# Seven block products instead of eight in the last 512 tokens of a gated MLP, with paired memory units and rewritten instruction orders

## The chip, the cores and the metric

The kernel runs on one core of a Trainium2 chip. The metric is device time in microseconds for one execution. Before the change the median of three runs is 672.04 us (671.85 to 672.40).

## What is computed

Attention over 4 batches and 8 heads (576 tokens, 64 dimensions a head) is mixed with a read from a memory matrix; the result, 2304 tokens by 512, goes through a gated MLP with no nonlinearity:

```python
local = np.matmul(softmax(causal(q @ k.T / 8)), v)
q_p = phi(q)                                   # x > 0 ? x + 1 : exp(x)
mem_out = (q_p @ M_prev) / (q_p @ z_prev + 1e-6)
x = g * mem_out + (1 - g) * local              # to 2304 x 512
out = ((x @ w_a) * (x @ w_b)) @ w_out          # 512 -> 1536 -> 512
```

The weights are given in 64 bits; the kernel makes of each a high and a low part of 32 bits in the form that one matmul pass takes, and every product of the MLP is three matmuls: high by high, high by low, low by high.

## The kernel before

Engines are called PE (matmuls), DVE, ACT, POOL (GpSimd) and SP (which issues the DMAs). The first 200 us are attention. Its steps, and the conversion of the weights, follow an order written out as text (HEAD, LOOP, TAIL: a step's name and the number of its pair of heads or column). BANKS says which bank of PSUM each step gets. Attention writes its part of x to DRAM (`xs`).

The MLP goes by blocks of 384 tokens (`TB`, six blocks, t = 0 to 5) and by 12 slices f of 128 of the 1536 hidden units; a pair (t, f) is a column. `hidden(c, 0)` makes 128 hidden rows of `x @ w_a` for 384 tokens in one PSUM bank, 12 matmuls of 384 columns (four slices of 128 of the 512 inputs, three matmuls each, `half`, L907), and `hidden(c, 1)` the same for `w_b`. `product` multiplies the two and splits the result: `cx` (ACT copies one from PSUM, L919), `mx` (DVE multiplies, L922), `hh` (ACT, high part, L926), `hl` (DVE, low part, L192). `outer` adds the slice to the output rows, 128 tokens at a time: 9 matmuls of 512 columns (L944). `written` copies finished rows out of PSUM and stores them.

From column 30 (`CUT`) on the order is a loop: `hidden(c, 0)`, matmuls of a memory unit, `hidden(c, 1)`, the four product steps, `outer` of the column before. Blocks 3 to 5 get their memory part from `memory_unit`, one for each of four pairs of heads, every third column: loads of q and xs, some ten operations on DVE, `sums` on POOL (L1098), `retrieve` on PE (L1106), `join` and the split of x into `xhl[t % 2]`.

```python
        for kk in range(KK):
            w0 = (n * KK + kk) * P
            for w, x in ((wh, xh), (wh, xl), (wl, xh)):
                nc.tensor.matmul(
                    pp, lhsT=w[:, w0:w0 + P], rhs=x[:, kk, :],
```

Of the kernel before, what the change touches and what calls it, by code (L numbers as in the profile page):

```python
# [8 lines left out]
F32 = mybir.dt.float32  # L9
# [12 lines left out]
Dk.0 zq.1 id.0 zq.0 zi.0 Dq.0 wm.14 TK.0 TQ.0 thK.0 ms.0 mk.0 ib.0 Dk.1 thQ.0 b_3.0 TK.1 b_2.0 Dq.1  # L22
Ek.1 tlK.0 Ek.0 tlQ.0 S_2.0 S_3.0 TQ.1 thK.1 b_.0 Eq.0 m2A.0 S_.0 e2A.0 thQ.1 sq.0 tlK.1 m2B.0 Tq.0
e2B.0 m3B.0 e3B.0 Tq.1 m3A.0 thq.0 mA.0 eA.0 tlq.0 Lv.0 thq.1 S_4.0 tlQ.1 b_2.1 S_2.1 Lt.2 mB.0 m4.0
e3A.0 eB.0 b_3.1 e4.0 m2A.1 Lk.2 S_3.1 m2B.1 v_h.0 b_.1 v_l.0 S_.1 tlq.1 r_.0 m3B.1 n2.0 ma.2 G2A.0
S_4.1 TQ.2 e2B.1 e2A.1 mb.2 mA.1 TK.2 mB.1 n4.0 e3B.1 n0.0 Lt.3 n1.0 mu.2 Lv.1 h2A.0 eB.1 eA.1 thQ.2
G0.0 l2A.0 G5.0 m4.1 m3A.1 tlQ.2 n3.0 v_h.1 h5.0 G2B.0 h0.0 thK.2 be.0 w_0.0 G4.0 l5.0 tlK.2 Lk.3
e3A.1 Tq.2 G3B.0 ga.0 h2B.0 l2B.0 thq.2 tlq.2 h4.0 G3A.0 G1.0 h3B.0 h1.0 l4.0 Lk.4 l3B.0 l0.0 l1.0
Lv.2
"""  # L30
BANKS = """
0123450125014152304513450415230145320451402554213054210530125502341502315413255124035124350342553201
4532045140255421305421053015220531405321041053451053420315402403123403125014320520145120145304215035
# [12 lines left out]
TK V2A b_ e3A pc tlQ b_2 r_ thK S_2 py m3B hl m2A S_ xA e3B V1B Tq m2B e2A clamp1 n1 hi1 n2 V2B Lt
mag0 e2B shift1 n4 thq mA shift2 eA md G2B G2A n3 xB shift0 G5 tlK lo0 H1 G1 LM G4 h5 clamp2 mB h2B
tlq n0 mc high1 h2A mb h1 l5 h4 pd l2B mag1 S_4 G0 l2A v_h l1 h0 G3A G3B Lk l4 eB w_0 pa l0 clamp0
low2 H0 mu m4 h3B Lp l3B lo1 Lv low0
# [3 lines left out]
v_l.12 h3A.11 pe.11 l3A.11 b_3.13 px.10 S_3.13 TQ.14 pf.11 e4.12 r_.12 n4.12 V1A.11 n0.12 pb.12  # L53
V2A.11 px.11 m3B.13 TK.14 b_.13 n3.12 thQ.14 b_2.13 e3B.13 pc.12 n1.12 tlQ.14 Lv.14 S_2.13 xA.11
S_.13 V1B.11 G0.12 pd.12 m3A.13 V2B.11 G5.12 thK.14 m2A.13 e3A.13 e2A.13 m2B.13 n2.12 mA.13 G1.12
e2B.13 eA.13 Lp.13 h0.12 py.11 st_.10 tlK.14 G3A.12 xB.11 h1.12 mB.13 TQ.15 G4.12 S_4.13 pe.12
h3A.12 G2A.12 b_3.14 py.10 l1.12 h5.12 S_3.14 w_0.12 l3A.12 G3B.12 l5.12 v_h.13 m4.13 eB.13 h4.12
pf.12 l4.12 l0.12 V1A.12 pa.13 h2A.12 G2B.12 l2A.12 m3A.14 V2A.12 Tq.15 e4.13 thQ.15 v_l.13 h3B.12
m3B.14 r_.13 n4.13 e3A.14 b_.14 S_.14 l3B.12 e3B.14 Lp.14 tlQ.15 pb.13 pc.13 px.12 h2B.12 n2.13
b_2.14 S_2.14 n3.13 V1B.12 mA.14 thq.15 Tq.14 xA.12 l2B.12 m2B.14 eA.14 e2B.14 TK.15 V2B.12 Lv.15  # L60
thq.14 mB.14 thK.15 G4.13 pd.13 m2A.14 n0.13 G5.13 G0.13 tlq.15 pe.13 tlq.14 G3A.13 e2A.14 xB.12
h5.13 tlK.15 l5.13 py.12 S_4.14 pf.13 n1.13 h0.13 G2A.13 h4.13 h3A.13 v_h.14 eB.14 h2A.13 l4.13
w_0.13 G1.13 l0.13 fw.0 h1.13 m4.14 l3A.13 G3B.13 b_3.15 l2A.13 px.13 e4.14 S_3.15 l1.13 v_l.14
h3B.13 m3B.15 r_.14 G2B.13 V1A.13 l3B.13 h2B.13 n2.14 st_.11 e3B.15 l2B.13 m3A.15 V2A.13 b_2.15
# [36 lines left out]
q_phi.3 ucx.21 uA.23 q_sums.1 umx.21 uhh.21 q_turn_h.2 q_phi2.3 q_join.1 q_norm.3 q_turn_l.2
q_join_h.1 ucx.22 uhl.21 q_join_l.1 uB.23 q_retrieve.2 q_norm2.3 Ml.3 q_norm3.3 umx.22 uhh.22 uhl.22
# [1179 lines left out]
```

## Time and profile before

| what | us |
|---|---|
| runs shown, median of three | 672.04 |
| the profiled execution | 671.25 |
| its span | 669.5 |
| PE busy | 657.8 (98%) |
| DVE, ACT, POOL busy | 437.5, 321.5, 235.8 |
| chain that ended last: L907, L944 | 44%, 22% |

The profile is of one execution. A line such as L907 is a line of the kernel; durations of matmuls overlap, so that the distance from one start to the next is what a stream of them costs.

### The profile page before, as it was taken

How to read it: one execution, taken by the hardware profiler on the slowest of the kernel's cores; microseconds unless marked ns; L12 is line 12 of the kernel's file. 1: busy time of each engine (PE TensorE's matmuls, PEld its weight loads, DVE VectorE, ACT ScalarE, POOL GpSimd, SP SyncE). 2: the span in 40 equal slices, each digit the busy share in tenths (PEclk: the TensorE clock that was granted, in tenths of full speed). 3: DMA queues.
4: the chain of work that ended last, by engine and by line, in shares of the span. 5: the costliest groups of instructions: out<-in, count | busy, mean ns of one | idle time of the engine just before them, and what ended most of it. 6: DMA issues, size and time to landing. Idle time of an engine off the chain costs nothing.

```text
span 669.5 us, 11351 instructions
## 1 busy us (share of the span) xinstructions
PE 657.8 (98%) x4110; PEld 606.3 (91%) x4110; DVE 437.5 (65%) x900; ACT 321.5 (48%) x765; POOL 235.8 (35%) x354
## 2 busy tenths in 40 slices
PE   8999999999989999999999999999999999999997
PEld 6889899999978999999899999999999999999996
DVE  6999998888799898887867434564444455422121
ACT  6999999999875445453323222232213212221111
POOL 4999999999992222124013110000000100000000
PEclk9999999999999999999999999999999999999999
DMA  8967576472923364633233121031110310010001
GB/s 188 198 136 184 133 190 182 124 176 79 338 93 131 126 205 172 189 95 83 68 72 97 34 60 39 1 96 36 30 31 31 88 37 1 0 48 1 0 1 47
DMA packets 124663, 64.24 MB, mean 96 GB/s; under 512 B 97856, under 2 KB 116288, under 8 KB 124608
## 3 DMA queue, kind: packets, MB, share of 16 engines
q1 hardware_dynamic: 124608, 63.53, 35.3%
q8 instruction: 32, 0.52, 0.3%
q14 instruction: 23, 0.19, 0.1%
HBM read 49.35 MB, written 14.16 MB: 95 GB/s over the span
## 4 chain that ended last, share of the span: by engine, by line
PE 84%; POOL 9%; DVE 2%; ACT 2%; issue 1%; SPq 1%; DMA 0%; POOLq 0%; DVEq 0%; ACTq 0%
PE pp L907 44%; PE o L944 22%; PE pt L188 6%; PE pw L702 5%; POOL P L602 4%; PE pt L536 4%; PE m L1106 1%; PE pw L536 1%; POOL vh L192 1%; ACT P L585 1%; POOL vh L477 1%; PE pt L907 1%; SPq L426 1%; POOL PT L192 1%; POOL xx L324 1%
## 5 line engine op out<-in xcount | busy, mean ns | idle before, releaser
L907 PE MATMUL pp<-xh,wh 128*128 128x384 f32 x568 | 190.8, 336 | 1.5 <-ACT xo L711 0.8
L907 PE MATMUL pp<-xh,wl 128*128 128x384 f32 x568 | 190.7, 336 | 0.0
L907 PE MATMUL pp<-xl,wh 128*128 128x384 f32 x568 | 190.2, 335 | 0.0
L922 DVE TENSOR_TENSOR x<-pp,x 128x384 f32<-128x384 f32 x71 | 39.4, 554 | 117.6 <-ACT x L919 117.5
L907 PEld LDWEIGHTS pp<-xh,wh 128*128 128x128 f32 x568 | 106.6, 188 | 5.0 <-ACT x L919 1.1
L919 ACT ACTIVATE x<-pp 128x384 f32<-128x384 f32 x71 | 34.6, 488 | 155.7 <-PE pp L907 140.4
L907 PEld LDWEIGHTS pp<-xl,wh 128*128 128x128 f32 x568 | 106.7, 188 | 2.8
L907 PEld LDWEIGHTS pp<-xh,wl 128*128 128x128 f32 x568 | 106.6, 188 | 0.0
L1098 POOL TENSOR_TENSOR xx<-xx 128x384 f32<-128x384 f32 x16 | 17.0, 1062 | 212.0 <-DMA xx<-xs 202.8
L944 PE MATMUL o<-wh,hl 128*128 128x512 f32 x216 | 85.2, 395 | 0.0
L944 PE MATMUL o<-wl,hh 128*128 128x512 f32 x216 | 85.0, 394 | 0.0
L602 POOL TENSOR_SCALAR P<-P,sum 128x384 f32<-128x384 f32 (+4 forms) x144 | 83.5, 600 | 4.4 <-DVE sum L594 4.2
L944 PE MATMUL o<-wh,hh 128*128 128x512 f32 x216 | 85.0, 394 | 0.0
L585 ACT ACTIVATE P<-pt,nm 128x384 f32<-128x384 f32 (+3 forms) x128 | 67.1, 534 | 5.4 <-DVE nm L575 4.8
L192 DVE TENSOR_TENSOR PT<-pt,PT 128x512 fp32r<-128x512 f32 (+2 forms) x112 | 62.3, 585 | 9.3 <-ACT PT L657 7.9
L702 PE MATMUL pw<-PT,vh 128*128 128x320 f32 (+4 forms) x416 | 63.8, 295 | 0.7 <-ACT xo L711 0.3
L926 ACT ACTIVATE hh<-x 128x384 fp32r<-128x384 f32 x72 | 37.6, 523 | 51.5 <-DVE x L922 40.9
L702 PEld LDWEIGHTS pw<-PT,vh 128*128 128x128 f32 x416 | 57.9, 189 | 4.8 <-issue 1.7
L192 DVE TENSOR_TENSOR hl<-x,hh 128x384 fp32r<-128x384 f32 x71 | 42.6, 600 | 29.7 <-ACT hh L926 29.5
L575 DVE TENSOR_REDUCE nm<-pt 128x1 f32<-128x128 f32 (+3 forms) x128 | 55.7, 478 | 4.2 <-PE pt L536 4.2
L657 ACT ACTIVATE PT<-pt 128x512 fp32r<-128x512 f32 (+2 forms) x112 | 52.5, 528 | 2.7 <-PE pw L702 1.4
L188 PE MATMUL pt<-ident,P 128*128 128x128 f32 (+1 forms) x400 | 52.2, 276 | 1.6 <-POOL P L602 1.2
(126 smaller groups left out, 1026.2 us busy)
## 6 DMA issues: line engine op xcount, KB each, us to landing
xs<-xo SPq DMA_DIRECT2D x16, 576.0 KB, 4.2
xx<-xs SPq DMA_DIRECT2D x48, 192.0 KB, 3.4
wr<-in_moe_w_a_dram SPq DMA_DIRECT2D x12, 512.0 KB, 3.8
wr<-in_moe_w_b_dram SPq DMA_DIRECT2D x12, 512.0 KB, 5.1
wr<-in_moe_w_out_dram SPq DMA_DIRECT2D x12, 512.0 KB, 4.2
out_dram<-ob SPq DMA_DIRECT2D x18, 256.0 KB, 2.1
qr<-in_q_dram SPq DMA_DIRECT2D x34, 128.0 KB, 3.1
kr<-in_k_dram SPq DMA_DIRECT2D x32, 128.0 KB, 2.9
```

The source lines that it names most:

```text
L188: nc.tensor.transpose(out, x, ident[0:x.shape[0], 0:x.shape[0]])
L192: eng.tensor_tensor(out=lo, in0=x, in1=hi, op=ALU.subtract)
L575: nc.vector.tensor_reduce(out=s["nm"][:, c:c + 1], in_=src, axis=AX.X, op=ALU.min)
L585: nc.scalar.activation(out=s["P", i][:, h, :], in_=src, func=AF.Exp, scale=-1.0, bias=s["nm"][:, c:c + 1], accum_out=s["sums"][:, c, 0:1],)
L602: nc.gpsimd.tensor_scalar(out=pr[:, h, :], in0=pr[:, h, :], scalar1=r[:, c:c + 1], scalar2=1.0, op0=ALU.mult, op1=ALU.mult,)
L657: nc.scalar.activation(out=dst, in_=src, func=AF.Copy)
L702: nc.tensor.matmul(pv[:, a:hi], lhsT=w, rhs=x, start=(n == 0), stop=(n == len(ops) - 1))
L907: nc.tensor.matmul(pp, lhsT=w[:, w0:w0 + P], rhs=x[:, kk, :], start=(c == 0), stop=(c == 3 * KK - 1),)
L919: nc.scalar.activation(out=x, in_=ps[1], func=AF.Copy)
L922: nc.vector.tensor_tensor(out=h[0], in0=ps[0], in1=h[0], op=ALU.mult)
L926: nc.scalar.activation(out=h[1], in_=h[0], func=AF.Copy)
L944: nc.tensor.matmul(po[t, m], lhsT=hx[:, m * P:(m + 1) * P], rhs=w[:, w0:w0 + DM], start=(f == 0 and n == 0), stop=(f == NFT - 1 and n == 2),)
```

## The change

The last 768 tokens are cut otherwise: block 4 has 256 tokens, and the last 512 are treated as two halves of 256 (`START`, `WIDTH`, `TH` = 256). For each slice f of those 512, the inputs are halved too, so that `[a; b] = [[A11, A12], [A21, A22]]` by `[[B11, B12], [B21, B22]]`, A of `w_a` and `w_b`, B of x; `step7` makes the four blocks of the result from seven products with sums of blocks. The sums of x (T1, TT2, T3, T4) are made once, in the columns of block 4 (`arrange`). The sums of weights (S1 to S4) are made for each f: `weight_whole` adds high and low parts, `weight_store` puts the whole weights into DRAM (`ws`, in TAIL's order), `sums_load` brings them back, `sums_of` adds on POOL, `sums_split` makes high and low parts.

```diff
+    START = [0, TB, 2 * TB, 3 * TB, 4 * TB, 4 * TB + TH, 4 * TB + 2 * TH]
+    WIDTH = [TB] * 4 + [TH] * 3
+    NB = 5
+    ws = [dram.tile([P, 4 * 2 * P], F32, name=f"ws{f}") for f in range(NFT)]
...
+    SUMS = {T1: (B12, B11), TT2: (B22, T1), T4: (B21, TT2), T3: (B22, B12)}
...
+    def weight_whole(n):
+        f, k = divmod(n, 2)
+        t = whole[n] = pools["ob"].tile([P, 2 * Q], F32, tag="ob", name="fw")
+        wh, wl = (w[:, 2 * k * Q:2 * (k + 1) * Q] for w in wt[f])
+        nc.vector.tensor_tensor(out=t, in0=wh, in1=wl, op=ALU.add)
...
+            a11, a12, a21, a22 = (ring[f][:, i * Q:(i + 1) * Q] for i in range(4))
+            for o, x, y, op in (
+                (a22, a21, a22, ALU.add), (a21, a11, a21, ALU.subtract),
+                (a11, a22, a11, ALU.subtract), (a12, a12, a11, ALU.subtract),
+            ):
+                nc.gpsimd.tensor_tensor(out=o, in0=x, in1=y, op=op)
...
+    def step7(f):
+        def part(o, w, x, first=False):
+            (wh, wl), (xh, xl) = w, xc[x]
+            for kk in range(2):
+                for a, b in ((wh, xh), (wh, xl), (wl, xh)):
+                    nc.tensor.matmul(
+                        o, lhsT=a[:, kk * P:(kk + 1) * P], rhs=b[:, kk, :],
...
+        if f:
+            prev[0]()
+        al = bank("ab")
+        part(al, a11, B11, True)
+        p1 = pools["w2"].tile([P, TB], F32, tag="x", name="x", bufs=1)[:, 0:TH]
+        nc.scalar.activation(out=p1, in_=al, func=AF.Copy)
+        if f:
+            prev[1]()
+        be = bank("ab2")
+        part(be, s2, TT2, True)
+        nc.vector.tensor_tensor(out=u2, in0=be, in1=p1, op=ALU.add)
+        if f:
+            prev[2]()
...
+        ga = bank("ab")
+        part(ga, s1, T1, True)
+        part(al, a12, B21)
+        part(be, s3, T3)
+        nc.vector.tensor_tensor(out=u3, in0=be, in1=p1, op=ALU.add)
+        nc.vector.tensor_tensor(out=u3, in0=u3, in1=ga, op=ALU.add)
+        if f:
+            sums_split(f + 1)
+            sums_load(f + 3)
+        prev[3]()
+        part(be, a22, T4)
+        nc.vector.tensor_tensor(out=h1, in0=be, in1=p1, op=ALU.add)
+        nc.vector.tensor_tensor(out=h1, in0=al, in1=h1, op=ALU.mult)
...
+        hh(0, h1)
+        if f < NFT - 1:
+            prev[4]()
+        hl(0, h1)
+        sums_of(f + 2)
+        part(ga, s4, B22)
...
+        def both():
+            nc.vector.tensor_tensor(out=u2, in0=ga, in1=u2, op=ALU.add)
+            nc.vector.tensor_tensor(out=u3, in0=u2, in1=u3, op=ALU.mult)
...
+        last["h"] = (both, lambda: hh(1, u3), lambda: hl(1, u3), lambda: out_rows(0), lambda: out_rows(1))
...
+    AT = range(36, 48, 2)
+    rest = (4, 0), (4, 2), (5, 0), (6, 0), (6, 2), (5, 2)
...
-        done(len(columns) - 1)
+            arrange(c)
+        for f in range(NFT):
+            step7(f)
```

(`prev` is the step before: its product of the second half, and its output rows.) A memory unit of the last 768 tokens takes two pairs of heads and 256 tokens (`rest`), one every second column from column 36 on. HEAD, BANKS, LOOP and TAIL are written anew throughout; two lines of TAIL show what is new in it:

```diff
+q_norm3.1 uc.17 q_turn.1 q_sums.0 q_join.0 q_phi.2 uB.19 uA.20 uB.21 Wf.0 Wf.1 ucx.19 q_turn_h.1
+umx.19 uhh.19 q_turn_l.1 uhl.19 Wf.2 uo.18 q_x_load.1 q_phi2.2 uo.19 q_norm.2 Ml.2 q_norm2.2
```

PE near the end, before: a column's second half ends and the output rows of the column before follow (`pp` is a hidden bank, `o` the output rows, `xh`, `xl`, `wh`, `wl` and `hh`, `hl` high and low parts).

```order
L907 MATMUL pp<-xh_72,wh_4556 128x384
L907 MATMUL pp<-xl_73,wh_4556 128x384
L907 MATMUL pp<-xh_72,wl_4557 128x384
L944 MATMUL o_7305<-wh_4471,hh 128x512
L944 MATMUL o_7305<-wl_4472,hh 128x512
L944 MATMUL o_7305<-wh_4471,hl 128x512
L944 MATMUL o_7309<-wh_4471,hh 128x512
L944 MATMUL o_7313<-wh_4471,hh 128x512
```

PE near the end, now: the first matmul of each product of one step, and of each group of output rows (of the step before) between them; every product has six matmuls, every group of rows three. `sh` is the high part of S2 to S4, `xeh` that of T3.

```order
L1270 MATMUL pp<-xh_84,wh_4552 128x256
L1270 MATMUL pp<-xh_84,sh 128x256
L1270 MATMUL pp<-xh_84,wh_4552 128x256
L1270 MATMUL pp<-xh_82,wh_4552 128x256
L1270 MATMUL pp<-xeh,sh 128x256
L1342 MATMUL o_7433<-wh_4520,hh 128x512
L1342 MATMUL m<-wh_4520,hh 128x512
L1270 MATMUL pp<-xh_82,wh_4552 128x256
L1342 MATMUL o_7453<-wh_4520,hh 128x512
L1342 MATMUL o_7457<-wh_4520,hh 128x512
L1270 MATMUL pp<-xh_82,sh 128x256
```

Two hidden products of 12 matmuls became seven of 6, and the output rows stand in two groups between the fifth and sixth and the sixth and seventh product.

DVE at the same place, before: two operations for a column.

```order
L922 TENSOR_TENSOR x<-pp,x 128x384
L192 TENSOR_TENSOR hl<-x,hh 128x384
```

DVE now, one step, from the first use of the second bank on (`u` and `h` are sums of banks, `sl` and `wl` low parts of the sums of weights of the next step).

```order
L1290 TENSOR_TENSOR u_7581<-pp,x 128x256
L201 TENSOR_TENSOR hl<-u_7515,hh 128x256
L1301 TENSOR_TENSOR u_7603<-pp,x 128x256
L1302 TENSOR_TENSOR u_7603<-u_7603,pp 128x256
L201 TENSOR_TENSOR sl<-xf,sh 128x768
L201 TENSOR_TENSOR wl_4083<-xf,wh_4082 128x256
L1309 TENSOR_TENSOR h_7625<-pp,x 128x256
L1310 TENSOR_TENSOR h_7625<-pp,h_7625 128x256
L201 TENSOR_TENSOR hl<-h_7625,hh 128x256
L1330 TENSOR_TENSOR u_7581<-pp,u_7581 128x256
L1331 TENSOR_TENSOR u_7603<-u_7581,u_7603 128x256
```

The two operations of a column became eleven, and the low parts of the weight sums stand ahead of the two that read the first bank for the last time (L1309, L1310).

DVE while block 2 is in work (t = 2), now: additions that rebuild weights (`fw`) stand between the operations of columns (L939, L201 `hl`) and of memory units (`ph`, `q`).

```order
L1215 TENSOR_TENSOR fw<-wh_4334,wl_4335 128x512
L939 TENSOR_TENSOR x<-pp,x 128x384
L201 TENSOR_TENSOR hl<-x,hh 128x384
L1092 TENSOR_SCALAR ph<-ph 128x384
L1095 SCALAR_TENSOR_TENSOR ph<-q_5298,ph 128x384
```

Before, no `fw` stands there; 24 of them are new.

## Rows read from the trace of the kernel before

**Rows 1.** The page: busy time by engine, PE's busy tenths and clock.

```profile
PE 657.8 (98%) x4110; PEld 606.3 (91%) x4110; DVE 437.5 (65%) x900; ACT 321.5 (48%) x765; POOL 235.8 (35%) x354
PEclk9999999999999999999999999999999999999999
```

**Rows 2.** Waits of PE in the span: total us, times, longest.

```profile
PE pt L188 <- POOL P L602: 1.2, 2, 0.8
...
PE m L1106 <- DVE yl L192: 0.4, 1, 0.4
...
PE pt L188 <- ACT P L657: 0.3, 1, 0.3
```

**Rows 3.** Stretches: length, then PE, PEld, DVE, ACT, POOL busy, PEclk, DMA share, GB/s.

```profile
300.00:350.00 50.00, 49.56 (x263) 46.06 (x262) 37.84 (x85) 15.19 (x31) 10.14 (x13) 1.00 0.31 73
350.00:400.00 50.00, 50.00 (x262) 46.40 (x261) 25.98 (x57) 13.74 (x29) 9.95 (x12) 1.00 0.26 65
500.00:650.00 150.00, 150.00 (x792) 140.24 (x791) 54.68 (x121) 32.77 (x66) 3.03 (x3) 1.00 0.08 23
```

**Rows 4.** The chain that ended last, its end: start, us, what.

```profile
654.66 2.10 PE o L944 x9
656.76 4.18 PE pp L907 x24
```

**Rows 5.** Groups by line, shapes apart, 500 to 650 us: busy us, mean ns.

```profile
L907 PE MATMUL pp<-xh,wh 128*128 128x384 f32 x186 | 62.4, 336 | 0.0
...
L922 DVE TENSOR_TENSOR x<-pp,x 128x384 f32<-128x384 f32 x24 | 13.3, 556 | 67.8 <-ACT x L919 67.8
```

**Rows 6.** PE's timeline at 102 us: start us, us, instruction.

```profile
102.10 0.42 PE L536 MATMUL pw<-f,f 128*128 128x288 f32 x2
102.37 0.29 PE L536 MATMUL pw<-f 128*128 128x288 f32 x1
102.50 0.43 PE L536 MATMUL pw<-f,f 128*128 128x288 f32 x2
```

**Rows 7.** PE's timeline at 447 us, a memory unit's retrieval.

```profile
446.68 0.27 PE L1106 MATMUL m<-yl,md 128*128 128x192 f32 x1
446.79 0.39 PE L1106 MATMUL m<-yh,md 128*128 128x192 f32 x2
447.01 0.28 PE L1106 MATMUL m<-yl,md 128*128 128x192 f32 x1
```

**Rows 8.** Groups by line on DVE, whole span, shapes apart.

```profile
L192 DVE TENSOR_TENSOR PT<-pt,PT 128x512 fp32r<-128x512 f32 x64 | 42.1, 680 | 2.7 <-ACT PT L657 2.2
...
L192 DVE TENSOR_TENSOR wl<-wt,wh 128x1024 fp32r<-128x1024 f32 x12 | 14.8, 1232 | 2.0 <-ACT wh L891 1.8
...
L192 DVE TENSOR_TENSOR f<-pt,f 128x192 fp32r<-128x192 f32 x16 | 5.5, 348 | 0.3 <-ACT f L512 0.3
```

**Rows 9.** The same on POOL.

```profile
L192 POOL TENSOR_TENSOR PT<-P,PT 128x256 fp32r<-128x256 f32 x16 | 11.7, 734 | 1.3
```

**Rows 10.** The same on ACT.

```profile
L657 ACT ACTIVATE P<-pt 128x256 f32<-128x256 f32 x16 | 6.1, 382 | 0.5 <-PE pt L188 0.5
```

**Rows 11.** DMA issues on the page: KB each, median us to landing.

```profile
wr<-in_moe_w_a_dram SPq DMA_DIRECT2D x12, 512.0 KB, 3.8
...
wr<-in_moe_w_out_dram SPq DMA_DIRECT2D x12, 512.0 KB, 4.2
out_dram<-ob SPq DMA_DIRECT2D x18, 256.0 KB, 2.1
```

**Rows 12.** Timeline near the end: PE goes on, ACT reads its bank.

```profile
660.78 0.39 PE L944 MATMUL o<-wh,hh 128*128 128x512 f32 x1
...
660.98 0.49 ACT L919 ACTIVATE x<-pp 128x384 f32<-128x384 f32 x1 [4.64 <-PE pp L907]
```

**Rows 13.** Timeline at 448 us: a POOL addition and a DVE subtraction.

```profile
448.36 1.01 POOL L1098 TENSOR_TENSOR xx<-xx 128x384 f32<-128x384 f32 x1 [31.11 <-DMA xx<-xs]
448.64 1.15 DVE L192 TENSOR_TENSOR xl<-xx,xh 128x384 fp32r<-128x384 f32 x1 [0.59 <-ACT xh L1116]
```

More of the change, by code (lines that the diff above doesn't have):

```diff
@@ L111 @@
+umx.29 Ws.20 uhh.29 uhl.29 q_join_h.4 q_join_l.4 uo.28 q_join_l.5 Wf.22 Ws.22 Wf.23 q_x_load.6 Ws.23
+Ws.17
 """
@@ L934, with outer @@
     po = {}
-    def outer(t, f, h):
+    def outer(t, f, h, ms=None):
         wh, wl = wt[f]
         w0 = 2 * KK * P
-        for m in range(TPB):
+        for m in ms or range(WIDTH[t] // P):
             if f == 0:
@@ L988, in column @@
         if f == NFT - 1:
-            for m in range(TPB):
+            for m in range(WIDTH[t] // P):
                 written(t, m)
     UNIT = (
-        "load phi phi2 norm norm2 norm3 turn turn_h turn_l sums retrieve join join_h join_l"
+        "load x_load phi phi2 norm norm2 norm3 turn turn_h turn_l sums retrieve join join_h join_l"
     )
@@ L1065, in norm2 @@
             half, whole, other = (
[L1066 removed]
+                pool.tile([P, J * U, 1], F32, tag=f"n{i}", name=f"n{i}", bufs=2) for i in range(3)
             )
[L1068 removed]
+            nc.vector.reduce_sum(out=half.rearrange("p u o -> p (u o)"), in_=tall(qz), axis=AX.X)
             for c in range(4):
@@ L1123, in memory_unit @@
             for f in (
-                load, phi, phi2, norm, norm2, norm3, turn, turn_h, turn_l, sums,
+                load, x_load, phi, phi2, norm, norm2, norm3, turn, turn_h, turn_l, sums,
                 retrieve, join, join_h, join_l,
@@ new lines, in split_x, with weight_store @@
+    def split_x(*os):
+        for o in os:
+            x = xf[0][:, PLACE[o]]
+            nc.scalar.activation(out=xc[o][0], in_=x, func=AF.Copy)
+            split_lo(nc.vector, xc[o][1], x, xc[o][0])
+    whole = {}
+    def weight_whole(n):
[3 more added lines that the diff above has]
+        nc.vector.tensor_tensor(out=t, in0=wh, in1=wl, op=ALU.add)
+    def weight_store(n):
+        f, k = divmod(n, 2)
+        nc.sync.dma_start(out=ws[f][:, 2 * k * Q:2 * (k + 1) * Q], in_=whole.pop(n))
@@ new lines, in sums_load, with sums_of @@
+    def sums_load(f):
+        if f < NFT:
+            a = 0 if f % 2 and f > 1 else 2
+            t = ring[f] = xf[0][:, a:a + 2].rearrange("p a b c -> p (a b c)")
+            nc.sync.dma_start(out=t, in_=ws[f])
+    def sums_of(f):
+        if f < NFT:
+            a11, a12, a21, a22 = (ring[f][:, i * Q:(i + 1) * Q] for i in range(4))
[4 more added lines that the diff above has]
+                nc.gpsimd.tensor_tensor(out=o, in0=x, in1=y, op=op)
@@ new lines, in sums_split @@
+    def sums_split(f):
+        if f >= NFT:
+            return
+        t = ring[f]
+        if f % 3 == 2:
+            two = [w[:, 0:3 * Q] for w in wt[0]]
+        else:
+            two = [pools["ring"].tile([P, 3 * Q], F32R, tag=f"s{f % 3}{n}", name="s" + n) for n in "hl"]
+        ring[f] = two, [w[:, 2 * Q:3 * Q] for w in wt[f]]
+        for (hi, lo), x in zip(ring[f], (t[:, 0:3 * Q], t[:, 3 * Q:4 * Q])):
+            nc.scalar.activation(out=hi, in_=x, func=AF.Copy)
+            split_lo(nc.vector, lo, x, hi)
@@ new lines, in last_rows, with arrange @@
+    def last_rows(m):
+        t, f = columns[-1]
+        outer(t, f, cols[len(columns) - 1][1][1:], (m,))
+        written(t, m)
+    def arrange(c):
+        at = c - 4 * NFT
+        if at == 0:
+            pieces()
+            split_x(B11)
+        if at == 1:
+            combine(T1)
+            split_x(T1)
+        if at == 2:
+            combine(TT2)
+            split_x(TT2)
+        if at == 3:
+            combine(T3)
+        if at == 4:
+            split_x(B21)
+            combine(T4)
+        if at == 5:
+            memb.close()
+            md.close()
+            for key, n in ("xe", 1), ("ring", 1), ("u", 1), ("ob", 2):
+                pool(mlp_r, key, "right", n)
+            xc[T3] = [
+                pools["xe"].tile([P, 2, TH], F32R, name=f"xe{n}") for n in "hl"
+            ]
+            split_x(T3)
+            sums_load(0)
+        if at == 6:
+            sums_of(0)
+        if at == 7:
+            sums_split(0)
+            sums_load(1)
+        if at == 8:
+            sums_of(1)
+        if at == 9:
+            sums_split(1)
+            sums_load(2)
@@ L1133, with planned @@
     columns += [(t, f) for t in range(2, NB) for f in range(NFT)]
+    ROWS = UNIT.split()
     plan, units, made = {}, {}, set()
-    for t in range(3, NB):
-        for j in range(KK):
-            c = (t - 1) * NFT + 3 * j
-            late = (
-                (-1, "load"),
-                (0, "phi phi2 norm norm2 norm3 turn turn_h turn_l sums"),
-                (2, "retrieve join join_h join_l"),
-            )
-            for o, names in late:
-                plan.setdefault((c + o, o == 2), []).extend((t, j, nm) for nm in names.split())
+    def planned(t, j, *when):
+        for c, mid, a, z in when:
+            plan.setdefault((c, mid), []).extend((t, j, nm) for nm in ROWS[a:z])
+    for j in range(KK):
+        c = 2 * NFT + (0, 3, 6, 8)[j]
+        planned(3, j, (c - 1, False, 0, 2), (c, False, 2, 11), (c + 2, True, 11, 15))
+    AT = range(36, 48, 2)
+    rest = (4, 0), (4, 2), (5, 0), (6, 0), (6, 2), (5, 2)
+    for n, (t, j) in enumerate(rest):
+        c = AT[n]
+        for o, mid, what in (
+            (-3 if n else -2, True, "load"), (-1 if n else 0, False, "phi phi2 norm norm2"),
+            (0, False, "x_load"), (0, False, "norm3 turn turn_h turn_l"), (1, False, "sums"),
+            (2, True, "retrieve join"), (2, False, "join_h join_l" if t < NB else ""),
+        ):
+            plan.setdefault((c + o, mid), []).extend((t, j, nm) for nm in what.split())
     def unit_step(t, j, nm):
@@ L1165 @@
         does = weights()
-        late, early, tiles, first, mlp_l, mlp_r, w4, second = (ExitStack() for _ in range(8))
+        late, early, tiles, first, mlp_l, mlp_r, w4, second, memb, md = (ExitStack() for _ in range(10))
         def pool(stack, key, side="left", bufs=1, **kw):
@@ L1246 @@
             memory(c, False)
-        done(len(columns) - 1)
-        for m in range(TPB):
-            written(NB - 1, m)
+            arrange(c)
+        last["h"] = None, None, None, lambda: last_rows(0), lambda: last_rows(1)
+        for f in range(NFT):
+            step7(f)
+        for go in last["h"]:
+            go()
         mlp_r.close()
```

364 lines of the change are left out of this document (234 added, 130 removed).

## The prediction

> **What bounds the kernel now.** I read the page's busy times and its forty slices first, then the waits of PE, then the table of stretches, then the chain of waits at the end, and last the groups by line and single instructions for durations. PE is busy 98% of the span at full clock [rows 1], but a busy PE is not yet the bound, so the waits decide: there are eleven kinds of wait of PE for another engine or a transfer, the first of 1.2 us, the last of 0.3 us, together 6.7 us, and after 225 us only one of 0.4 us is left [rows 2]. The other engines have room late: between 500 and 650 us PE is busy all of the 150 us, DVE 54.7, ACT 32.8 and POOL 3.0 [rows 3]. The chain at the end says the same: matmuls alone, 24 of the first kind (L907) in 4.18 us, then 9 of the second (L944) in 2.10 us [rows 4]. So the MLP is a queue of matmuls, and its time is their number by their pitch. A matmul over 384 columns costs 4.18 / 24 = 0.174 us, one over 512 costs 2.10 / 9 = 0.233 us. The durations in the groups by line are longer, 336 ns where the pitch is 174 [rows 5], because matmuls overlap; they may not be added up.
>
> **Matmuls of the last 768 tokens.** Up to token 1536 the columns have the same shapes. Before, the rest is two blocks of 384: 2 x 12 x 24 = 576 matmuls of 384 columns, 576 x 0.174 = 100.3 us. Now it is a block of 256 (12 x 24 = 288 matmuls of 256 columns) and twelve steps of seven products with six matmuls each (504), so 792 of 256 columns. The matmuls of the output rows stay 216 of 512 columns: 2 x 12 x 9 before, 12 x 6 + 12 x 12 now. All hangs on the pitch at 256 columns, which the trace of before does not show for a stream of equal ones. Per column the pitch is 0.174 / 384 = 0.454 ns and 0.233 / 512 = 0.456 ns; two matmuls of 288 columns start 0.27 us before the next, 0.131 to 0.135 each [rows 6]; that too is 0.46 ns a column. By columns 256 costs 0.117 us. Below it lies a floor: 192 columns take 0.11 us, not 0.087 [rows 7], so something besides columns, which I take to be the load of the next weights, needs 0.11 us. The floor is under 0.117, so I take 0.117; the ends are 0.111 (nearest row below) and 0.132 (nearest above). 792 x 0.117 = 92.7 us: **7.6 us less**, between 12.4 less and 4.2 more.
>
> **Retrieval.** Before, blocks 4 and 5 cost 24 matmuls of 192 columns and 12 of 384: 2.6 + 2.1 = 4.7 us. Now the block of 256 has 12 of 192 and 12 of 64, all at the floor of 0.11, and the two halves of the last 512 tokens 24 of 256: 2.6 + 2.8 = 5.4 us. **0.7 us more.**
>
> **What one step asks of the others.** PE needs 42 x 0.117 + 12 x 0.233 = 7.7 us a step. DVE does nine operations of 256 columns, 0.42 us each by the rows of 192 and 384 columns (0.348, 0.556), and the low parts of the weight sums, 768 columns at 0.96 (between 0.680 for 512 and 1.232 for 1024) and 256 at 0.42 [rows 5, 8]: 5.2 us. POOL's four sums cost 0.73 each [rows 9], 2.9 us. ACT copies 256 columns three times at 0.38 [rows 10] and splits 1024 more, under 3 us. The load of 512 KB lands after about 4 us [rows 11], while it is issued more than a step ahead. So no engine is full; what can hurt is order. I follow a step from the start of its first product at 0:
>
> - The fifth product (S3 by T3) ends at 3.5 us. Its reader can begin 0.2 us after PE has gone on, as ACT's copy does in the present columns [rows 12]. DVE then has u3 twice (to 4.6), the low parts of 768 and 256 columns (to 5.9), and h1 twice (to 6.8, with the sixth product ended at 5.6).
> - PE meanwhile does six output matmuls, the sixth product, six output matmuls and the seventh product: until 7.7 us. The next step's first product overwrites the bank that h1 read at 6.8. **Spare: 0.9 us.** This is the tightest place; every other bank has over 0.7 us, with nothing but its own operation queued ahead on DVE.
>
> POOL is the doubt. The load of step f+3 is issued when DVE has read the low parts of f+1 (5.9), lands near 2.2 of the next step, and POOL's sums then run to about 5.2, across the place where DVE makes low parts. The trace shows what happens there: a DVE subtraction from two SBUF tiles that takes 0.56 us alone started 0.28 us into a POOL addition and took 1.15 us, to 0.42 us after the addition's end [rows 13]. The Trainium skill (SBUF — State Buffer, the section on the engine side and its shared pair) says that DVE with two SBUF inputs and GpSimd take a pair of ports by exclusive lock for a whole instruction; the trace agrees, in that one pair. From the row alone: each of the two low parts can wait for one POOL addition, at most 0.73 us: together 1.46 us against 0.9 us spare, or up to 0.56 us a step. Mostly POOL is nearly done and one is hit in its middle, within the spare; I take 0.1 us a step for eleven steps: **1.1 us more**, ends 0 and 6.2.
>
> **What else moves.** The 24 additions that rebuild whole weights for DRAM cost DVE 24 x 0.68 = 16 us [rows 8] in columns 19 to 30, about 335 to 405 us (6.3 us a column, back from the end). DVE was idle 12.2 and 24.0 us in the two stretches of 50 us that hold most of it [rows 3], so they are covered; were DVE full, PE would meet the waits of [rows 2], a few tenths each. Their 24 stores and the 12 loads go on SP's queue, ahead of later loads of q and x; the DMA engines are 31% and 26% busy there [rows 3], and a store of 256 KB lands in 2.1 us [rows 11]. Memory units come in pairs every second column, at most 10 of 12.5 us of DVE's time, columns included (about eleven operations of 512 columns at 0.68 and smaller ones, plus two columns with two of 0.56). The sums and halves of x (T1, TT2, T3, T4) lie in columns of 24 x 0.117 + 6 x 0.233 = 4.2 us, of which DVE, with two operations of 512 columns, two of 256 and the waits for ACT between them, needs about 3.3. For some ten changes of bank or group in each step I allow 0.3 us over all. At the end the chain both, hh, hl (2.0 us) hides behind six output matmuls and two of the last six (1.9 us): 0.1 us. The orders of the attention stage are written anew with the same work; I count nothing, with ends of 6.7 us either way: all waits of [rows 2] gone, or as many again.
>
> **Sum.** -7.6 + 0.7 + 1.1 + 0.3 + 0.1 = -5.4 us. The profiled execution took 671.25 us, with a span of 669.5; that makes 665.9. The median of the runs shown is 672.04, 0.8 above the profiled one: **666.6 us**.
>
> **Rivals.**
>
> 1. *The attention order gains too.* Up to 6.7 us of waits could go. For it: those waits are few, and sit at the start and where attention ends. Against: the tail of attention lists nearly the same matmuls. Half of it gives 663. Chance 0.14.
> 2. *POOL's lock costs every step its full price.* Spare 0.9 us, need 1.46: 6.2 us instead of 1.1, so 671.7. It is what the lock of the Trainium skill (SBUF — State Buffer, the same section) would do at its worst. It decides only if both low parts meet a fresh addition; for it, the load lands just then, against it, POOL needs 2.9 of 7.7 us. If half that, 669. Chance 0.12.
> 3. *Matmuls of 256 columns are not cheap (the other side).* If the load of 128 columns of weights, not the stream, sets the pitch here, the gain turns at (100.3 - 2.2) / 792 = 0.124 us, 2.2 us being the other terms of the sum; at 0.132 the result is 672.04 + 4.2 + 2.2 = 678.4. Place: all 792 matmuls. For it, the floor at 192 columns; against, 288 columns already run by columns. Chance 0.06.
> 4. *The new order costs, or the change is starved.* If attention waits as much again, or DVE between 335 and 405 us lets PE wait, the time is 666.6 + 3 to 7 = 670 to 673. For it, four engines nearly full until 200 us; against, none of the work changed. Chance 0.12.
>
> The forecast keeps 0.56, for 664 to 669.5.
>
> **Numbers.** A measurement here can tell about 0.2%, 1.3 us. Faster by more (under 670.7): the forecast, rival 1 and half of 2 and a third of 4, 0.80. Within: 0.08. Slower (over 673.4): rival 3 and part of 4, 0.12. The range reaches from rival 1 with much of its gain, 661.5, to the middle of rivals 2 and 4, 673; outside are rival 3, the ends of 1 and 4.
>
> **What would show it.** Pitch: a product of six matmuls in 0.70 us, a step in 7.7 to 7.8 us, twelve steps in 93. Lock: DVE's low part of 768 columns longer than 0.96 us, and PE waiting for h1 (L1310) at the first product of a step. Order: PE's waits before 225 us near 6.3 us, and the columns of 384 tokens starting as before. I am wrong if the steps take 8.2 us or more, if the pitch at 256 columns is 0.124 or more, or if the time before the last 768 tokens moves by over 3 us.

## The result, and the profile after

The changed kernel takes **666.0 us** (median of 5 runs, 665.53 to 666.85); the kernel before took 671.85 us on the same chip (671.55 to 672.4). The ratio is 0.9914, 95% interval 0.9899 to 0.9928: 0.86% faster. The forecast was 666.6 us, with a range of 661.5 to 673 and a chance of 0.80 for faster. The profiled execution took 666.34 us with a span of 664.2, 4.9 us less than the profiled one before (671.25).

First the page of the changed kernel, against [rows 1, 11]:

```profile
PE 652.4 (98%) x4338; PEld 600.9 (90%) x4338; DVE 499.0 (75%) x1012; ACT 333.2 (50%) x797; POOL 273.4 (41%) x400
PEclk9999999999999999999999999999999999999999
...
xf<-ws SPq DMA_DIRECT2D x12, 512.0 KB, 3.2
```

PE issues 228 matmuls more and is done sooner. DVE has 62 us more to do and POOL 38. The stretches of [rows 3] show where that went:

```profile
300.00:350.00 50.00, 50.00 (x265) 46.65 (x264) 45.12 (x96) 16.49 (x33) 10.43 (x13) 1.00 0.40 102
350.00:400.00 50.00, 50.00 (x264) 46.70 (x263) 35.29 (x71) 12.85 (x27) 9.78 (x11) 1.00 0.47 147
500.00:650.00 150.00, 150.00 (x1030) 139.65 (x1029) 84.57 (x179) 42.42 (x95) 37.76 (x49) 1.00 0.15 52
```

The waits of PE, against [rows 2] (what waited, for what, us in total, times, longest). Six more of 0.8 to 0.2 us are left out; together it is 6.9 us, and all of it lies before 225 us:

```profile
PE pt L397 <- DVE idle L755: 1.2, 1, 1.2
PE pt L197 <- POOL P L611: 1.0, 1, 1.0
PE pp L923 <- ACT xo L720: 0.8, 1, 0.8
PE pt L197 <- ACT P L594: 0.8, 2, 0.6
```

The chain of work that ended last, at the block of 256 tokens and in one of the twelve steps (start, us, what; L923 are products of a column, L1270 products of a step, L961 and L1342 output rows):

```profile
531.17 2.86 PE pp L923 x24
534.03 1.40 PE o L961 x6
535.43 2.86 PE pp L923 x24
...
625.71 4.29 PE pp L1270 x36
630.00 0.70 PE o L1342 x3
630.70 0.70 PE m L1342 x3
631.40 0.71 PE pp L1270 x6
632.11 1.40 PE o L1342 x6
633.51 4.29 PE pp L1270 x36
```

PE alone stands on it. A matmul of 256 columns costs 2.86 / 24 = 0.119 us in the columns of block 4 and 4.29 / 36 = 0.119 in the steps; a column takes 4.26 us (535.43 - 531.17), a step 7.80 (633.51 - 625.71). So the last 768 tokens cost 792 x 2.86 / 24 = 94.4 us in products instead of 100.3. An output matmul of 512 columns still costs 1.40 / 6 = 0.233.

Now DVE and POOL in the same step, and the first matmul of the next step on PE (timeline):

```profile
627.73 3.25 POOL L1236 TENSOR_TENSOR xf<-xf 128x256 f32<-128x256 f32 x4 [4.50 <-DMA xf<-ws]
...
630.49 0.42 DVE L1302 TENSOR_TENSOR u<-u,pp 128x256 f32<-128x256 f32 x1
630.83 0.96 DVE L201 TENSOR_TENSOR sl<-xf,sh 128x768 fp32r<-128x768 f32 x1
631.72 0.41 DVE L201 TENSOR_TENSOR wl<-xf,wh 128x256 fp32r<-128x256 f32 x1
632.15 0.42 DVE L1309 TENSOR_TENSOR h<-pp,x 128x256 f32<-128x256 f32 x1
632.61 0.42 DVE L1310 TENSOR_TENSOR h<-pp,h 128x256 f32<-128x256 f32 x1
...
634.05 0.28 PE L1270 MATMUL pp<-xh,wh 128*128 128x256 f32 x1
```

The place I called the tightest looks as forecast: h1 (L1310) ends at 633.03 (632.61 + 0.42), and the first product of the next step overwrites its bank at 634.05. The spare is 1.02 us, where 0.9 was predicted. POOL's four additions end at 630.98 and DVE's low parts begin at 630.83, so in this step the two hardly meet. Over the steps from 575 to 640 us they do meet. First the means of two of DVE's subtractions in the changed kernel, then the same in the run below that leaves out POOL's additions (it makes the low part of 768 columns twice):

```profile
L201 DVE TENSOR_TENSOR sl<-xf,sh 128x768 fp32r<-128x768 f32 x6 | 6.2, 1033 | 0.0
L201 DVE TENSOR_TENSOR hl<-u,hh 128x256 fp32r<-128x256 f32 x8 | 4.3, 539 | 0.0
```

```profile
L201 DVE TENSOR_TENSOR sl<-xf,sh 128x768 fp32r<-128x768 f32 x12 | 11.5, 955 | 0.2
L201 DVE TENSOR_TENSOR hl<-u,hh 128x256 fp32r<-128x256 f32 x8 | 3.4, 426 | 0.0
```

So POOL holds DVE up a little in the changed kernel too, by about 0.1 us at each of the two places (1033 - 955 and 539 - 426 ns). PE does not notice: the last operation of h1 (L1310) starts 7.80 us after the one before (609.21, 617.01, 624.81, 632.61 us), whether the low part of 768 columns took 1.08 or 0.96 us.

Order, last. A pair of columns in the middle stands where it stood: its output rows begin at 397.54 us in the changed kernel and at 397.51 in the kernel before. In front of it, though, single columns had moved by up to 5 us, and the copy of the second one came at 211.6 us instead of 210.7. I read that as a cost of the new order, 0.9 us, and set out to test it.

### The profile page after: what moved, and what is told of

Its sections match the earlier page's. It is cut to its first block, busy times and chain, and to the rows that moved or that the text cites. A ratio compares the mean times of both kernels' runs of the same rounds, so it can differ in the third digit from the quotient of the medians.

```text
span 664.2 us, 12217 instructions
## 1 busy us (share of the span) xinstructions
PE 652.4 (98%) x4338; PEld 600.9 (90%) x4338; DVE 499.0 (75%) x1012; ACT 333.2 (50%) x797; POOL 273.4 (41%) x400
## 4 chain that ended last, share of the span: by engine, by line
PE 81%; DVE 8%; SPq 3%; ACT 3%; DMA 2%; POOL 1%; issue 1%; ACTq 0%; DVEq 0%; POOLq 0%
PE pp L923 32%; PE o L961 16%; PE pp L1270 9%; PE pt L197 6%; PE pw L711 5%; PE pt L545 4%; PE o L1342 4%; DVE PT L201 3%; DVE nm L584 2%; SPq L1053 2%; POOL P L611 1%; PE m L1157 1%; PE m L1342 1%; PE pw L545 1%; ACT P L594 1%; DMA qr<-in_q_dram 1%
## 5 line engine op out<-in xcount | busy, mean ns | idle before, releaser
L923 PE MATMUL pp<-xh,wh 128*128 128x384 f32 (+1 forms) x472 | 153.7, 326 | 1.5 <-ACT xo L720 0.8
L923 PE MATMUL pp<-xh,wl 128*128 128x384 f32 (+1 forms) x472 | 153.5, 325 | 0.0
L923 PE MATMUL pp<-xl,wh 128*128 128x384 f32 (+1 forms) x472 | 153.2, 325 | 0.0
L923 PEld LDWEIGHTS pp<-xh,wh 128*128 128x128 f32 x472 | 88.9, 188 | 4.5 <-ACT x L936 1.2
L923 PEld LDWEIGHTS pp<-xl,wh 128*128 128x128 f32 x472 | 88.9, 188 | 2.4
L923 PEld LDWEIGHTS pp<-xh,wl 128*128 128x128 f32 x472 | 88.9, 188 | 0.0
L936 ACT ACTIVATE x<-pp 128x384 f32<-128x384 f32 (+1 forms) x59 | 27.5, 467 | 102.0 <-PE pp L923 86.7
L1236 POOL TENSOR_TENSOR xf<-xf 128x256 f32<-128x256 f32 x48 | 36.3, 757 | 99.7 <-DMA xf<-ws 55.3
L201 DVE TENSOR_TENSOR PT<-pt,PT 128x512 fp32r<-128x512 f32 (+2 forms) x112 | 62.7, 588 | 10.4 <-ACT PT L666 8.1
L594 ACT ACTIVATE P<-pt,nm 128x128 f32<-128x128 f32 (+3 forms) x128 | 66.8, 530 | 5.1 <-DVE nm L584 3.4
L939 DVE TENSOR_TENSOR x<-pp,x 128x384 f32<-128x384 f32 (+1 forms) x59 | 31.1, 527 | 48.2 <-ACT x L936 46.1
L961 PE MATMUL o<-wh,hl 128*128 128x512 f32 x168 | 66.3, 395 | 0.0
L961 PE MATMUL o<-wl,hh 128*128 128x512 f32 x168 | 66.3, 394 | 0.0
L961 PE MATMUL o<-wh,hh 128*128 128x512 f32 x168 | 66.2, 394 | 0.0
L866 POOL TENSOR_SCALAR wt<-wt 128x512 f32<-128x512 f32 (+1 forms) x21 | 21.0, 1000 | 83.8 <-ACT wt L860 83.8
L943 ACT ACTIVATE hh<-x 128x384 fp32r<-128x384 f32 (+1 forms) x60 | 30.1, 501 | 40.6 <-DVE x L939 31.2
```

The lines of the kernel that those rows point to most:

```text
L201: eng.tensor_tensor(out=lo, in0=x, in1=hi, op=ALU.subtract)
L594: nc.scalar.activation(out=s["P", i][:, h, :], in_=src, func=AF.Exp, scale=-1.0, bias=s["nm"][:, c:c + 1], accum_out=s["sums"][:, c, 0:1],)
L923: nc.tensor.matmul(pp, lhsT=w[:, w0:w0 + P], rhs=x[:, kk, :], start=(c == 0), stop=(c == 3 * KK - 1),)
L961: nc.tensor.matmul(po[t, m], lhsT=hx[:, m * P:(m + 1) * P], rhs=w[:, w0:w0 + DM], start=(f == 0 and n == 0), stop=(f == NFT - 1 and n == 2),)
L1236: nc.gpsimd.tensor_tensor(out=o, in0=x, in1=y, op=op)
```

## The experiments

**The order of attention, three runs.** In the first two, the tables of one kernel are put into the other, up to `uo.16`, the seventeenth column; in the third, only HEAD and its 30 banks. The start of the first edit:

```diff
 HEAD = """
-Dk.0 zq.1 id.0 zq.0 zi.0 Dq.0 wm.14 TK.0 TQ.0 thK.0 ms.0 mk.0 ib.0 Dk.1 thQ.0 b_3.0 TK.1 b_2.0 Dq.1
+id.0 zi.0 wm.14 mk.0 ib.0 Dk.0 zq.1 Dq.0 TK.0 TQ.0 zq.0 Dk.1 b_2.0 thK.0 Dq.1 Eq.0 tlK.0 TK.1 thQ.0
...
```

> The kernel before, with one thing of the change alone: the order of the attention stage and of the first 17 columns (HEAD, LOOP, BANKS, and TAIL up to uo.16). Against the kernel before, 671.85 us. Theory A, the new order costs what the second column's copy shows, which came at 211.6 us in the changed kernel and at 210.7 before: 672.8 us, ratio 1.0013, the copy near 211.6. Theory B, the order is worth nothing, as I predicted, and those 0.9 us come from something else in the changed kernel: 671.9 us, the copy near 210.7. Rival 1 of the prediction, the order gains: 670 or less.

Measured: 670.89 us, ratio 0.9982 (0.9973 to 0.9991), the copy at 211.1. Neither theory: the copy is later, yet the kernel is faster by 1 us (671.91 before, in the same runs). PE's waits fit that: 5.6 us in all, against 6.7 [rows 2]. The copy was a bad mark, since the new order does other work ahead of it.

> The changed kernel with the order of the kernel before in the attention stage and the first 17 columns, and its own order behind them. Against the changed kernel, 666.0 us. Theory A, the new order costs 0.9 us: 665.1 us, the second column's copy near 210.7, and this is then faster than both kernels. Theory B, the order is worth nothing: 666.0 us, the copy near 211.6. If the new order gains somewhere that the copy does not show: above 666.5.

Measured: 665.61 us (665.48 to 665.81), ratio 0.9903 (0.9890 to 0.9917), the copy at 210.8. The interval covers that of the changed kernel, so the two are not told apart. In the kernel before, the new order gains 1 us; in the changed one it loses 0.4 us or nothing. So the gain of the change is not this order's: with the old order, the rest of the change gives 6.3 us (671.91 - 665.61). This version has the lowest median of all that do the whole work.

> The changed kernel with the order of the kernel before in the first 129 steps of attention alone (HEAD, and the 30 banks that belong to it); the loop keeps the new order. Theory A1, the loss lies in the first 50 us, where PE loses 6.7 us against 6.0: 665.2 us, the second column's copy near 210.8. Theory A2, it lies in the loop and behind: 666.0 us, the copy near 211.6. Above 666.3: the two parts fit only each other.

Measured: 670.91 us, 4.9 us slower than the changed kernel, with waits of PE that are new or longer than in either kernel:

```profile
PE pt L545 <- DVE PT L201: 2.4, 1, 2.4
PE pt L197 <- ACT P L594: 1.9, 2, 1.7
PE pt L197 <- DVE PT L201: 1.4, 1, 1.4
```

These first 129 steps and this loop do not fit each other. Here a piece of an order had no worth of its own; other cuts were not tried.

**What a step can bear, four runs and a control.**

```diff
         for (hi, lo), x in zip(ring[f], (t[:, 0:3 * Q], t[:, 3 * Q:4 * Q])):
             nc.scalar.activation(out=hi, in_=x, func=AF.Copy)
             split_lo(nc.vector, lo, x, hi)
+            if lo.shape[1] > Q:
+                split_lo(nc.vector, lo, x, hi)
```

> The changed kernel with DVE's subtraction for the low parts of 768 columns done twice in each step: 1.0 us more of DVE ahead of h1, in all twelve steps. In the changed kernel h1 ends 1.02 us before the first product of the next step begins (625.23 and 626.25 in one step). Theory A, that is the whole spare of the step: 666.0, at most 666.5 us, and PE begins to wait for h1 or stands at the edge. Theory B, the spare of 0.9 us of my prediction: 0.1 us x 11 = 1.1, so 667.1. Theory C, the place tightens earlier than h1 shows, through POOL: 1 us x 11, so up to 677.

Measured: 671.1 us, 5.1 more than the changed kernel, and steps of 8.3 to 8.6 us, most of them 8.36. Theory C. The timeline of POOL and DVE in one step:

```profile
631.57 3.86 POOL L1236 TENSOR_TENSOR xf<-xf 128x256 f32<-128x256 f32 x4 [4.49 <-DMA xf<-ws]
...
633.75 2.48 DVE L201 TENSOR_TENSOR sl<-xf,sh 128x768 fp32r<-128x768 f32 x2
636.16 0.41 DVE L201 TENSOR_TENSOR wl<-xf,wh 128x256 fp32r<-128x256 f32 x1
```

And the one wait of PE behind 560 us:

```profile
PE pp L1272 <- DVE h L1312: 3.0, 8, 0.6
```

DVE's two subtractions take 2.48 us, not 1.9, and POOL's four additions 3.86, not 3.25. They meet: by their times, POOL's fourth addition (1.34 us where 0.73 is usual) waits for the first subtraction, and the second subtraction (1.38 us) for the addition. The next load is issued later too, since it waits for DVE's low parts, so POOL starts later in every step. To show that it is POOL, the same kernel without POOL's additions:

```diff
-                nc.gpsimd.tensor_tensor(out=o, in0=x, in1=y, op=op)
+                pass
```

> The run with the subtraction of 768 columns done twice (671.1 us, steps of 8.36 us), now without POOL's additions (the sums of weight blocks are left out, so the products use the blocks themselves). Theory A, POOL's fourth addition holds DVE up there and makes 0.5 us of each step: with it gone DVE has 1.0 us more work in a spare of 1.02, so steps of 7.80 to 7.85 and 666.0 to 666.6 us. Theory B, DVE's own work is what does not fit: steps of 8.3 us and 671.

Measured: 666.43 us, steps of 7.80 us, no wait of PE. The two subtractions now take 1.94 us:

```profile
630.97 1.94 DVE L201 TENSOR_TENSOR sl<-xf,sh 128x768 fp32r<-128x768 f32 x2
```

So the spare of 1.0 us is there as read: with 0.98 us of it used, h1 ends at 634.04 and the next product begins at 634.19. The 0.5 us and more that each step lost above is POOL's. This is the mechanism of rival 2, shown; in the changed kernel it costs DVE some 0.2 us a step, and PE nothing.

> The same with both subtractions done twice, 1.0 + 0.42 us more of DVE ahead of h1 in each step. Theory A, spare 1.02 us: PE waits 0.4 us in each of eleven steps, 4.4 us, so 670.4. Theory B, spare 0.9 us: 0.5 x 11 = 5.7, so 671.7. Theory C, h1 is not the tightest place of a step and more is spare: 666.0.

The edit repeats both `split_lo`. Measured: 676.69 us, steps of about 8.97, PE waiting for h1 7.8 us in all, in ten of the steps. All theories were too low, since they left the meeting with POOL out: 0.4 us of DVE work too much and 0.56 for the meeting, as in the run before, are 0.96 of the 1.17 us that a step lost. A part of the other 0.2 is a longer meeting: the two subtractions of 768 columns take 2.54 us on the average of the steps from 575 to 640 us, in the run before 2.45. The rest stays open.

```diff
             for o, x, y, op in (
+                (a22, a21, a22, ALU.add), (a22, a22, a21, ALU.subtract),
+                (a22, a21, a22, ALU.add), (a22, a22, a21, ALU.subtract),
                 (a22, a21, a22, ALU.add), (a21, a11, a21, ALU.subtract),
```

> The changed kernel with eight additions on POOL in each step instead of four (the first is done, undone, done, undone and done): 6.5 us of a step's 7.8, so that DVE's low parts always run beside POOL. Theory A, rival 2 of the prediction, DVE with two SBUF inputs waits for a whole POOL addition: the low parts take up to 1.7 and 1.15 us instead of 1.0 and 0.41, and with 1.02 us spare PE waits up to 0.44 us in each of eleven steps, up to 4.8 us: 667 to 671. Theory B, POOL does not hold DVE up enough to use the spare: 666.0, the low parts at most 0.4 us longer each. In both PE waits for nothing that was not already late.

Measured: 670.29 us (669.27 to 671.27). By the total alone that is theory A, but the steps stay at 7.80 us. Groups of DVE from 575 to 640 us:

```profile
L201 DVE TENSOR_TENSOR wl<-xf,wh 128x256 fp32r<-128x256 f32 x8 | 7.7, 957 | 0.0
L201 DVE TENSOR_TENSOR wl<-xf,wh 128x768 fp32r<-128x768 f32 x3 | 2.9, 965 | 0.0
```

The waits of PE behind 240 us:

```profile
PE o L961 <- ACT hh L943: 2.3, 1, 2.3
PE pp L1272 <- DVE u L1303: 0.5, 1, 0.5
```

The longest wait of ACT for POOL, between 530 and 575 us:

```profile
ACT sh L1251 <- POOL xf L1238: 9.4, 2, 6.5
```

The low part of 256 columns takes 957 ns instead of 414: it waits for POOL. The one of 768 columns ahead of it does not wait in seven of these eight steps. That eats 0.42 us of the spare of 1.02 (0.60 are left in most steps), and PE notices nothing. In the eighth step, at 635.69 us, both wait (1.48 and 0.96 us): h1 then ends at 638.83, and the next product begins at 638.91. So even the worst case of rival 2, met once, just fits into the spare. The time is lost earlier: ACT waits for POOL's first sums, with the copy hh of a column queued behind it, and PE waits 2.3 us for that. The first step begins 3.6 us later than in the changed kernel, the second 5.1, the last 4.9. So the lock takes its 0.5 us a step, as rival 2 had it, but in most steps once and not twice, and the spare holds it.

```diff
         part(ga, s4, B22)
+        part(ga, s4, B22)
```

> The changed kernel with an eighth product in each step (the seventh done twice, so the results are other ones): 6 matmuls of 256 columns more, 72 in all. Theory A, the steps are a queue of matmuls at 0.119 us: 72 x 0.119 = 8.6 us, so 674.6, and a step of 8.51 us. Theory B, something beside PE's queue takes part in the 7.80 us of a step: less than 8.6, down to 666.0. Theory C, a product costs more than its matmuls (the change of weights or bank): over 675.5.

Measured: 674.91 us, 8.9 more than the changed kernel, a step of 8.51 us (39.36 - 30.85 in the chain). Theory A:

```profile
630.85 4.99 PE pp L1270 x42
...
639.36 0.71 PE pp L1270 x6
```

A product saved is worth 0.71 us a step, and nothing else stands in the way.

**The pitch below and above 256 columns, two runs.**

```diff
+        last["f"] = f
...
+            n = (256, 224, 192, 128)[last["f"] // 3]
...
+                    m = TH if first and c == 0 else n
...
-                        o, lhsT=a[:, kk * P:(kk + 1) * P], rhs=b[:, kk, :],
+                        o[:, 0:m], lhsT=a[:, kk * P:(kk + 1) * P], rhs=b[:, kk, 0:m],
```

> The changed kernel with products of fewer columns: 256 in steps 0 to 2, 224 in 3 to 5, 192 in 6 to 8, 128 in 9 to 11 (the first matmul of a bank stays at 256; the columns left out are not computed). It is read for the pitch of matmuls inside a product. Theory A, at 256 columns the stream of columns sets the pitch, 0.119 / 256 = 0.465 ns a column: 0.104 at 224, 0.089 at 192, 0.060 at 128. Theory B, a floor of 0.11 us from the load of weights stands below it, as the 192 columns of the kernel before showed: 0.110 to 0.111 at 224, at 192 and at 128. Theory C, the floor already sets the 0.119 at 256: 0.119 at all four.

Measured, from the chain; the groups of six hold no matmul of full width (256, 224, 192 and 128 columns in this order):

```profile
576.51 0.71 PE pp L1273 x6
...
599.38 0.66 PE pp L1273 x6
...
621.92 0.65 PE pp L1273 x6
...
644.67 0.62 PE pp L1273 x6
```

That is 0.119, 0.110, 0.108 and 0.103 us; in the groups of 36, three of which are of full width, 0.111, 0.111 and 0.110 (from 4.03, 4.03 and 3.98 us). The low figures of the single groups are in part only moved: the six output matmuls behind the group take 1.45 us behind the 0.62 and 1.39 behind the 0.71, so (0.62 + 0.06) / 6 = 0.113. By the groups of 36, halving the columns takes 8% off. Theory B: a floor of 0.11 us, which 192 columns had shown [rows 7]. That it is the load of the weights, as theory B has it, this run does not show. The whole kernel gains but 2 us by it, 664.05.

> The changed kernel with the matmuls of 384 columns in blocks 2 and 3 cut to 352 columns for the first three columns of a block, then 320, 288 and 256, three each (the first matmul of a bank stays at 384; the columns left out are not computed). It is read for the pitch between two of equal width. Theory A, the stream sets the pitch all the way down and 256 has a small fixed addition: 0.174 / 384 = 0.454 ns a column, so 0.160 at 352, 0.145 at 320, 0.131 at 288, and 0.119 at 256 where 0.116 would be the line. Theory B, the pitch leaves the line gradually before it reaches the floor of 0.111: 0.161, 0.147, 0.134, 0.119. Theory C, 0.119 is peculiar to the last two stages (their banks, weights or neighbours), and 256 columns cost 0.116 here.

The same edit in `half` of the columns. Measured, from the chain (352 columns, then 320, 288, 256; one matmul in twelve has 384):

```profile
357.05 11.82 PE pp L925 x72
370.94 7.14 PE pp L925 x48
...
396.45 3.26 PE pp L925 x24
...
407.68 2.97 PE pp L925 x24
```

With the full ones at 0.174 taken out: (11.82 - 6 x 0.174) / 66 = 0.163, (7.14 - 4 x 0.174) / 44 = 0.146, (3.26 - 2 x 0.174) / 22 = 0.132, and 0.119. That is 0.46 ns a column throughout, a little above the 0.454 at 384 [rows 4]; theory A or B, which differ by 0.003 at most. Theory C falls: 256 columns cost 0.119 here too.

**The cover of the whole weights, two runs.**

```diff
-        nc.vector.tensor_tensor(out=t, in0=wh, in1=wl, op=ALU.add)
...
+        whole[n] = wt[f][0][:, 2 * k * Q:2 * (k + 1) * Q].bitcast(F32)
```

> The changed kernel without the 24 additions that rebuild whole weights (the high halves are stored, so the low halves are missing from the sums of blocks): DVE does 24 x 0.68 = 16.3 us less in columns 19 to 30. Theory A, they are covered, as predicted: 666.0 us, within 0.5. Theory B, DVE at 45.1 of 50 us from 300 to 350 us delays PE with them: 0.5 to 2 us faster, 664 to 665.5.

Measured: 665.95 us (664.98 to 666.34), no change. Theory A: without them DVE is busy 41.4 and 22.5 us in the two stretches of 50 from 300 to 400 us, with them 45.1 and 35.3, and PE doesn't notice.

```diff
-        nc.vector.tensor_tensor(out=t, in0=wh, in1=wl, op=ALU.add)
+        for _ in range(2):
+            nc.vector.tensor_tensor(out=t, in0=wh, in1=wl, op=ALU.add)
```

> The changed kernel with those 24 additions done twice, 16.3 us more of DVE between 335 and 405 us, where it is busy 53.5 of 70 us. Theory A, the cover holds on the whole, since 16.5 us were idle, though columns begin to wait: 666 to 668. Theory B, DVE is full there and what it lacks in single columns goes to PE: several us, 669 or more.

Measured: 675.05 us, 9 more. Theory B, though by the sum of busy times there was room. Waits of PE behind 240 us (two more of 1.0 and 0.9 us, for DVE too, are left out):

```profile
PE m L1157 <- DVE xx L1164: 3.3, 2, 1.9
PE pp L923 <- DVE xl L201: 2.0, 1, 2.0
```

A piece of the chain of work, which runs through DVE there:

```profile
327.25 0.60 DVE fw L1216
327.87 1.31 DVE fw L1216 x2
329.20 0.69 DVE fw L1216
329.90 0.47 DVE x L939
```

Four additions in a row (2.6 us) stand ahead of a column's product x on DVE, and PE soon waits. The cover is there once, not twice.

## Why the prediction was right, and where only its sum was

- **What bounds the kernel: right.** PE waits 6.9 us in all, nothing after 225 us, and 72 matmuls more (the eighth product) cost 8.9 us where their pitch gives 8.6.
- **Matmuls, -7.6 us: mis-sized.** The step that failed is "By columns 256 costs 0.117 us", which took the rate of 384 and 512 columns. At 256 it is 0.119, so 94.4 us and a gain of 5.9. The floor of 0.11 below it was right; so were its bounds. The allowance of 0.3 us for changes of bank and group was not needed beside it, as the steps of 7.80 us are (7.80 - 12 x 0.233) / 42 = 0.119.
- **Retrieval, +0.7 us: 0.9.** Before it took four pieces of 0.65 and four of some 0.52 us; now four of 0.71 and two of 1.26 to 1.5 for the block that lies across two sequences. The first begins as its low halves arrive and loses 0.25. This is read from the chain; no run takes the paired units out by themselves.
- **POOL's lock, +1.1 us: nothing that PE sees.** The load takes 3.2 us, not 4, and POOL's four sums 3.25, not 2.9; they end 4.7 us into the step (630.98 - 626.25) where 5.2 was forecast, close to the start of DVE's low parts. The 0.2 us a step that DVE still loses does not reach PE. The doubt was a real one: pushed together by 1 us of DVE work, the two cost each step 0.56 us, and without POOL's additions nothing. The Trainium skill (SBUF — State Buffer, section "SBUF: two separate sides") says that DVE with two SBUF inputs and a GpSimd instruction that reads SBUF hold a pair of ports by an exclusive lock, each for its whole instruction. The runs agree, in both directions: 957 ns instead of 414 for DVE, 3.86 us instead of 3.25 for POOL.
- **Cover of the whole weights: right,** with less reserve than the two idle figures of [rows 3] suggested. Of the sixteen microseconds added once, PE saw none, added twice nine.
- **The end, +0.1 us: right, with a term left out beside it.** The last six output matmuls take 1.48 us instead of 1.40, so the chain ahead of them costs 0.1 us. What follows the last matmul was not in the sum: its copy and store take 4.1 us (664.2 - 660.08), before 4.7 (669.5 - 664.76), so -0.6. Why they are shorter was not tried.
- **The order, 0: right** within 1 us, and rivals 1 and 4 with their 3 to 7 us are out. The last 768 tokens begin 0.4 us later than before, retrieval apart (512.82 us with 4.9 us of retrieval ahead of it, before 510.15 with 2.6). But for the ends I had no mechanism, only the sum of the waits. The run with a foreign head shows that a loss of 4.9 us was quite possible.

Summed again with these: -5.9 + 0.9 + 0.1 - 0.6 + 0.4 = -5.1 us, against -5.3 between the spans of the profiled pair, -4.9 between their times and -5.85 between the medians. So the 666.6 was near partly by luck: the matmuls gained 1.7 us less than I said, and against that the lock (1.1), the allowance (0.3) and the end (0.6) together cost 2.0 us less.

## What to carry to other kernels

Cost a queue of matmuls by their pitch in the chain, and measure that at the width you will use: fewer products of narrower blocks pay in full only as long as the width keeps off the floor, here 0.11 us for 224 columns and fewer. Read the spare of an operation from its end to the instruction that overwrites its bank, and then ask what else shifts if it is used up; here the first microsecond was free by itself, and it cost half a microsecond because DVE then met POOL. And a mark in a reordered kernel must have the same work ahead of it, or it shows the order and not the time.

## What the runs showed of the hardware

- A matmul here needs 0.46 ns a column from 512 columns down to 256 (0.233, 0.174, 0.163, 0.146, 0.132, 0.119 us at 512, 384, 352, 320, 288, 256), and then 0.11 us at 224, 192 and 128 (groups of 36, their three of 256 columns taken out).
- The wait between POOL and DVE goes both ways and adds up over a pair: two subtractions 2.48 us instead of 1.94 while four additions took 3.86 instead of 3.25. With POOL busy nearly throughout, the second of two low parts in a row was hit in all eight steps (957 ns instead of 414), the first, three times as wide, in one (1.48 us; in the others 0.95 to 0.99, as without POOL). I had expected each to wait. What decides which one is hit was not tried.
